# Dividing the first batch's attention output by its sums as it leaves PSUM, with TensorE spreading the reciprocals

## The chip, the core and the metric

The kernel runs on one core of one Trainium2 chip. The metric is the device time of one execution in microseconds (us); lower is better. The core's engines work side by side, each through its own queue in order: PE (TensorE, matrix products), DVE (VectorE), ACT (ScalarE), POOL (GpSimd) and SP (SyncE, which issues the transfers here). SBUF is the on-chip memory, PSUM the small memory that PE writes its results to.

## The reference

Attention with a sliding window and a few sink keys feeds a gated feed-forward network. There are 4 batches, 8 heads, 768 positions and 64 numbers per head.

```python
scores = scale * np.matmul(q, k.transpose(0, 1, 3, 2))
keep = is_sink | in_window                 # 4 sinks, a window of 128
scores = np.where(keep, scores, -1000000000.0)
scores = scores - np.max(scores, axis=-1, keepdims=True)
a = np.exp(scores)
a = a / (np.sum(a, axis=-1, keepdims=True) + 1e-09)
x = np.matmul(a, v)                        # heads side by side: 512 numbers
h = np.maximum(x @ w_in, 0.0)              # 1024 numbers
conv_out = ...                             # 3 taps along the sequence
gate = 1.0 / (1.0 + np.exp(-conv_out))
out = (h * gate) @ w_out
```

The weights w_in, conv_w and w_out come as 64-bit numbers and are narrowed on the chip.

## The kernel before

**Work and its order.** Heads go in pairs; g numbers the 16 pairs of all batches, four to a batch. A sequence has six query tiles of 128, in two halves (hf 0 and 1). The jobs of the first batch are the first halves of its four pairs, then their second halves: 24 steps of one query tile each. Per step the loop in `banded` calls `scores` for this tile, `transp` for the tile before and `pv` for the one two steps back, and between them takes pieces of feed-forward work (`fill`). The feed-forward network of the first 256 positions can start after the 12th step; from then on PE has such pieces between the attention work. One weight block per step, from step 2 to step 18, is narrowed and split (`m.need`). What each engine runs in which order is set in the end by the compiler's own scheduling pass, which reorders instructions within an engine.

**One query tile** (`scores`). PE makes the scores of both heads (tile sc in PSUM, two buffers). DVE puts in the mask and finds the row maximum (L502, L503), ACT takes the exponential into the tile pe and accumulates the row sums in sm (L506), DVE adds the sums up and takes their reciprocal (L508, L509), and POOL multiplies the probabilities by it, one instruction per head (L511). `transp` turns the scaled probabilities over on PE (pts, L526), ACT copies them out (pT, L528), POOL clears what lies outside the window (L530, L532).

**One half of a pair** (`pv`). PE adds the products of pT and the values into px (L567). The sink keys' probabilities of the three tiles, 16 columns for each head and tile (SP), are copied to sk by ACT (L539), turned over (tk, L540), copied to sT (L542) and multiplied with the sinks' values c.vs, into the same px (L570). `xout` writes x to SBUF in two parts whose sum is x: the high part xH by ACT (L345), the rest xL by DVE (L346). The later batches use other sink tiles and keep the scaling on POOL.

**A weight block** (`split`). `narrow` makes 32-bit numbers of the 64-bit ones (ACT L111, DVE L112, L113, L114; tiles stm, three buffers). ACT writes the high part (L121); the low part is a subtraction of two SBUF tiles (L122), for w_in on POOL, for w_out (wo0 to wo7) on DVE.

**Feed-forward.** `first` puts 12 products into ph (L183; the last three need x of the fourth pair), `gate` works on ACT, DVE (L195, L196, L198) and POOL (L200, L201), `second` adds to po (L210). The tag "h" of the PSUM pool has two buffers; ph, tk and the turned q and k tiles share it. In the first batch two SBUF tiles, roomH and roomL, lie where x of the second batch will be; roomH holds zeros and the sinks' values.

## Time and profile before

| | |
|---|---|
| median of 3 runs | 490.8 us (489.17 to 491.21) |
| the profiled execution | 491.53 us; its span is 489.8 us, so 1.73 us lie around the span |
| mean granted PE clock | 0.991 |
| busy over the span | PE 457.6, DVE 343.8, ACT 344.3, POOL 314.0 us |
| PE busy, first 12 us | 2.07 us (loading) |
| PE busy, 12 to 102 us | 76.78 of 90 us (first batch's attention, feed-forward from about 49 us) |
| PE busy, 120 to 360 us | 239.56 of 240 us |
| PE busy, 360 to 490 us | 122.15 of 130 us |

The profile lists every instruction with start and duration. A row "0.5 <-DVE sm L509" gives idle time and what ended it. A view by stages gives busy time of each engine in a stretch, the number of instructions in brackets, and the clock that PE was granted. Ends of matmuls are modelled, so a matmul's own duration is longer than the distance to the next one.

### The profile page before, as it was taken

What the parts mean: (1) busy time and instruction counts of PE and PEld (TensorE: products, weight loads), DVE (VectorE), ACT (ScalarE), POOL (GpSimd) and SP (SyncE); (2) the same over time, 40 slices, a digit from 0 to 9 for tenths busy, and PEclk for the clock granted to TensorE, in tenths of its full rate; (3) what the DMA queues carried; (4) which work ended last, traced back from release to release, by engine and by line L of the source; (5) the groups of instructions that cost most, each with busy time, mean ns of one, the idle gap of its engine ahead of it and who ended that gap; (6) DMA issues with size and microseconds to landing.
All of it is one profiled execution on the core that took longest, in us unless ns stands there. A gap on an engine that the chain in (4) does not pass through costs nothing.

```text
span 489.8 us, 10503 instructions
## 1 busy us (share of the span) xinstructions
PE 457.6 (93%) x3149; PEld 388.8 (79%) x3149; DVE 343.8 (70%) x1211; ACT 344.3 (70%) x1087; POOL 314.0 (64%) x614
## 2 busy tenths in 40 slices
PE   1877698999999999999999999999999999999993
PEld 1644577778888888998888887898888888999982
DVE  4689989857768777776677778686776574655561
ACT  3888877869867978887768877785867664545541
POOL 3396688856876868695657667585765564444341
PEclk9999979999999999999999999999999999999999
DMA  5687744547234141433231421333120100101001
GB/s 145 188 250 205 187 146 84 135 91 184 52 81 115 62 115 33 101 96 83 73 86 35 107 68 34 71 92 85 45 58 8 45 2 1 44 1 43 26 20 51
DMA packets 87307, 41.01 MB, mean 84 GB/s; under 512 B 80161, under 2 KB 80185, under 8 KB 87241
## 3 DMA queue, kind: packets, MB, share of 16 engines
q1 hardware_dynamic: 87240, 40.25, 32.0%
q8 instruction: 27, 0.44, 0.4%
q14 instruction: 40, 0.32, 0.2%
HBM read 27.60 MB, written 6.29 MB: 69 GB/s over the span
## 4 chain that ended last, share of the span: by engine, by line
PE 83%; POOL 4%; DVE 3%; ACT 3%; DMA 3%; issue 2%; SPq 1%; DVEq 0%; ACTq 0%; POOLq 0%
PE ph L183 28%; PE po L210 27%; PE px L567 8%; PE pts L526 4%; PE sc L337 4%; PE sc L338 3%; PE px L570 2%; PE tq L271 2%; POOL pe L511 2%; PE sc L334 2%; PE tk L289 1%; DMA raw<-in_k_dram 1%; POOL wiL L122 1%; DMA sc_i<-in_window_dram 1%; POOL pT L530 1%
## 5 line engine op out<-in xcount | busy, mean ns | idle before, releaser
L210 PE MATMUL po<-woH,g 128*128 128x512 f32 x384 | 142.2, 410 | 1.2 <-POOL g L200 1.2
L183 PE MATMUL ph<-xH,wiH 128*128 128x258 f32 (+1 forms) x384 | 112.7, 293 | 1.2 <-ACT sT L542 1.2
L183 PE MATMUL ph<-xH,wiL 128*128 128x258 f32 (+1 forms) x384 | 110.0, 287 | 0.0
L183 PE MATMUL ph<-xL,wiH 128*128 128x258 f32 (+1 forms) x384 | 109.4, 285 | 0.0
L511 POOL TENSOR_SCALAR pe<-pe,sm 128x132 f32<-128x132 f32 (+1 forms) x192 | 86.0, 459 | 30.4 <-DVE sm L509 19.1
L200 POOL TENSOR_SCALAR g<-t 128x256 fp32r<-128x256 f32 x96 | 41.9, 437 | 79.1 <-DVE t L198 59.0
L506 ACT ACTIVATE pe<-pe,sm 128x132 f32<-128x132 f32 (+1 forms) x192 | 77.5, 407 | 16.6 <-DVE sm L503 15.2
L195 DVE SCALAR_TENSOR_TENSOR t<-hb,cw,t 128x256 f32<-128x256 f32 x96 | 55.5, 579 | 35.5 <-ACT t L194 34.4
L210 PEld LDWEIGHTS po<-woH,g 128*128 128x128 f32 x384 | 69.0, 189 | 12.1 <-POOL g L200 2.6
L183 PEld LDWEIGHTS ph<-xH,wiH 128*128 128x128 f32 x384 | 73.2, 191 | 6.6 <-ACT sT L542 2.0
L201 POOL TENSOR_TENSOR g<-t,g 128x256 fp32r<-128x256 f32 x96 | 74.3, 774 | 5.4
L210 PE MATMUL po<-woL,g 128*128 128x512 f32 x192 | 76.6, 399 | 0.0
L183 PEld LDWEIGHTS ph<-xH,wiL 128*128 128x128 f32 x384 | 73.3, 191 | 2.2
L183 PEld LDWEIGHTS ph<-xL,wiH 128*128 128x128 f32 x384 | 73.3, 191 | 0.9
L197 ACT ACTIVATE t<-t 128x256 f32<-128x256 f32 x96 | 40.3, 420 | 34.7 <-DVE t L196 34.4
L502 DVE COPY_PREDICATED sc<-before,sc 128x128 f32<-128x128 int32 x160 | 44.9, 291 | 25.7 <-PE sc L338 20.5
L198 DVE SCALAR_TENSOR_TENSOR t<-t,hb 128x256 f32<-128x256 f32 x96 | 47.0, 490 | 21.1 <-ACT t L197 20.2
L503 DVE CUSTOM_DVE_ANT_0 pe<-sc,m 128x132 f32<-128x132 f32 (+1 forms) x192 | 52.6, 288 | 10.1 <-PE sc L338 7.8
L196 DVE SCALAR_TENSOR_TENSOR t<-hb,cw,t 128x256 f32<-128x256 f32 x96 | 55.6, 579 | 4.4
L530 POOL TENSOR_SCALAR_AFFINE_SELECT pT<-pT 128x256 f32<-128x256 f32 x80 | 39.2, 490 | 29.5 <-ACT pT L528 25.2
L190 ACT ACTIVATE hb<-ph 128x258 f32<-128x258 f32 (+1 forms) x96 | 37.0, 385 | 29.3 <-PE ph L183 27.8
L194 ACT ACTIVATE t<-hb,cw 128x256 f32<-128x256 f32 x96 | 49.2, 513 | 7.1 <-POOL g L201 3.3
(123 smaller groups left out, 918.4 us busy)
## 6 DMA issues: line engine op xcount, KB each, us to landing
raw<-in_q_dram SPq DMA_DIRECT2D x64, 96.0 KB
raw<-in_k_dram SPq DMA_DIRECT2D x64, 96.0 KB
out_dram<-stm SPq DMA_DIRECT2D x24, 256.0 KB
kk<-kk SPq DMA_DIRECT2D x24, 198.0 KB
vraw<-in_v_dram SPq DMA_DIRECT2D x24, 192.0 KB
wi_0r<-in_moe_w_in_dram SPq DMA_DIRECT2D x2, 512.0 KB
wi_1r<-in_moe_w_in_dram SPq DMA_DIRECT2D x2, 512.0 KB
wi_2r<-in_moe_w_in_dram SPq DMA_DIRECT2D x2, 512.0 KB
```

The costliest lines, as they stand in the source:

```text
L183: nc.tensor.matmul(u.h[:, 0:W], w[:, cc, ff * P:(ff + 1) * P], x[:, cc, t0:t1], start=(i == 0), stop=(i == len(prods) - 1))
L194: nc.scalar.mul(a, prev, cw[:, 0, ff:ff + 1])
L195: nc.vector.scalar_tensor_tensor(out=e, in0=this, scalar=cw[:, 1, ff:ff + 1], in1=a, op0=ALU.mult, op1=ALU.add)
L196: nc.vector.scalar_tensor_tensor(out=a, in0=nxt, scalar=cw[:, 2, ff:ff + 1], in1=e, op0=ALU.mult, op1=ALU.add)
L198: nc.vector.scalar_tensor_tensor(out=a, in0=e, scalar=1.0, in1=this, op0=ALU.add, op1=ALU.mult)
L201: nc.gpsimd.tensor_tensor(out=u.g[:, 1], in0=a, in1=f(u.g[:, 0]), op=ALU.subtract)
L210: nc.tensor.matmul(po[:, 0:c.DM], u.g[:, a, tt * P:(tt + 1) * P], w[:, ff, :], start=(ff == 0 and i == 0), stop=(ff == NFF - 1 and i == 2))
L502: nc.vector.copy_predicated(pc[:, KW:SW], before.bitcast(I32), pc[:, 0:P])
L503: nc.vector.tensor_tensor_reduce(out=pe[:, j, cols], in0=pc[:, P:SW][:, cols], in1=mk, op0=ALU.add, op1=ALU.min, scale=1.0, scalar=3.0e38, ...
L506: nc.scalar.activation(pe[:, j, cols], pe[:, j, cols], AF.Exp, bias=sm[:, j:j + 1], scale=-1.0, accum_out=sm[:, 2 + 2 * j:3 + 2 * j])
L511: nc.gpsimd.tensor_scalar(pe[:, j, cols], pe[:, j, cols], sm[:, 8 + j:9 + j], 1.0, ALU.mult, ALU.mult)
L530: nc.gpsimd.affine_select(out=keytile(g, t - 1, hf)[:, :, 1], in_=own, pattern=[[0, 2], [-1, P]], compare_op=ALU.is_gt, fill=c.zero, base= ...
```

## The change

For the first batch (g below 4) only:

- `scores` no longer multiplies the probabilities on POOL (L511, 48 instructions). The reciprocals are written as a fifth column beside the four sink columns of sk (SP is 5 instead of 16), one column for each head and tile, so sk has 30 columns instead of 96.
- sk is turned over as before; sT then holds, besides the sinks' unscaled probabilities, the reciprocals of the three tiles along the free axis. A constant c.sel (made once by ACT in roomL) has ones in those rows that belong to the reciprocals of one tile. Three further products of c.sel and sT per half put into rb, a PSUM tile of tag "h", the reciprocal for each of the 128 rows of px and each position: 24 matmuls.
- `xout` copies rb to a part of roomL by ACT, DVE multiplies px by it into the same place, and xH and xL are made from there instead of from px: per half one ACT and one DVE instruction more.
- The rows of c.vs that are not sinks are zero, so the reciprocal columns add nothing to px.

For all weights: the low parts of wo0 to wo7 are subtracted on POOL instead of DVE.

```diff
-SP = 16
+SP = NS + 1
...
-                out.append((f"wo{ff}", ..., lambda raw, ff=ff: self.split(..., self.c.nc.vector)))
+                out.append((f"wo{ff}", ..., lambda raw, ff=ff: self.split(..., self.c.nc.gpsimd)))
...
-    def xout(self, g, half, px):
+    def xout(self, g, half, px, rb=None):
...
+        if rb is not None:
+            n = 384 * (1 + g % 2)
+            r = c.room[:, n:n + 384]
+            nc.scalar.copy(r, rb)
+            nc.vector.tensor_tensor(out=r, in0=px, in1=r, op=ALU.mult)
+            px = r
         nc.scalar.copy(xH[:, hp, s], px)
         nc.vector.tensor_tensor(out=xL[:, hp, s], in0=px, in1=f(xH[:, hp, s]), op=ALU.subtract)
...
+    c.room = m.room[1]
+    c.sel = m.room[1][0:6 * SP, 0:3 * P].rearrange("r (w p) -> r w p", w=3)
+    nc.scalar.copy(c.sel.rearrange("r w (j d) -> r (w j) d", j=2),
+                   c.ident[0:6 * SP, NS:6 * SP:SP].rearrange("r (n o) -> r n o", o=1).to_broadcast([6 * SP, 6, D]))
...
         nc.vector.tensor_reduce(out=sm[:, 6:8], ...)
+        if g < NPAIR:
+            if u == 0:
+                s.sk[hf] = ap.tile([P, 6, SP], F32, tag="sk", name=f"sk{g}_{hf}")
+            nc.vector.reciprocal(s.sk[hf][:, 2 * u:2 * u + 2, NS], sm[:, 6:8])
+            return
         nc.vector.reciprocal(sm[:, 8:10], sm[:, 6:8])
...
-                sk = ap.tile([P, 6, SP], F32, tag="sk", name=f"sk{g}_{hf}")
-                nc.scalar.copy(sk, sinks[:, :, 0:SP])
+                sk = s.sk[hf]
+                nc.scalar.copy(sk[:, :, 0:NS], sinks[:, :, 0:NS])
...
-        A.xout(g, hf, px)
+        rb = None
+        if g < NPAIR:
+            rb = m.ps.tile([P, 3 * P], F32, tag="h", name=f"rb{g}_{hf}", bufs=2)
+            for w in range(3):
+                nc.tensor.matmul(rb[:, P * w:P * w + P], c.sel[:, w], s.sT, start=True, stop=True, skip_group_check=True)
+        A.xout(g, hf, px, rb)
```

The change shifts line numbers by 6 to 20; L511 of before is L526 after, L530 and L532 are L545 and L547, L502 and L503 are L512 and L513, L346 is L352.

The order of the instructions moves with it. In the rows below the last number of a name is a buffer's number, and "0" or "1" ahead of it the half. First, POOL's queue while the first halves of the first batch run, before; pe are probabilities, wiL and woL low parts of weights, pT the turned probabilities:

```order
L122 TENSOR_TENSOR wiL<-stm_329,wiH 128x512
L511 TENSOR_SCALAR pe_0_421<-pe_0_421,sm_160 128x128 x2
L511 TENSOR_SCALAR pe_0_421<-pe_0_421,sm_161 128x132 x2
L122 TENSOR_TENSOR wiL<-stm_380,wiH 128x512
L530 AFFINE_SELECT pT_0_0_355<-pT_1_0_406 128x2x128
L493 MEMSET pe_0_545 128x2x4
L530 AFFINE_SELECT pT_1_0_406<-pT_2_0_437 128x2x128
L511 TENSOR_SCALAR pe_0_421<-pe_0_421,sm_162 128x132 x2
L532 AFFINE_SELECT pT_1_0_406<-pT_1_0_406 128x2x128
L532 AFFINE_SELECT pT_2_0_437<-pT_2_0_437 128x2x128
```

The same stretch of POOL's queue after:

```order
L122 TENSOR_TENSOR wiL<-stm_323,wiH 128x512
L122 TENSOR_TENSOR wiL<-stm_378,wiH 128x512
L545 AFFINE_SELECT pT_0_0_347<-pT_1_0_402 128x2x128
L503 MEMSET pe_0_541 128x2x4
L547 AFFINE_SELECT pT_1_0_402<-pT_1_0_402 128x2x128
L545 AFFINE_SELECT pT_1_0_402<-pT_2_0_432 128x2x128
L547 AFFINE_SELECT pT_2_0_432<-pT_2_0_432 128x2x128
L122 TENSOR_TENSOR woL<-stm_448,woH 128x512
L545 AFFINE_SELECT pT_0_0_472<-pT_1_0_527 128x2x128
L547 AFFINE_SELECT pT_1_0_527<-pT_1_0_527 128x2x128
L122 TENSOR_TENSOR woL<-stm_503,woH 128x512
```

The scalings are gone, and subtractions of w_out stand between the window clearings.

Second, DVE's queue where the first pair's second half ends and the second pair's begins, before; sc are scores, t the gate's tiles, sm the sums:

```order
L195 SCALAR_TENSOR_TENSOR t_802<-hb_114,cw,t_801 128x256
L112 TENSOR_SCALAR stm_704<-stm_705 128x512
L502 COPY_PREDICATED sc_3_0_827<-before,sc_3_0_827 128x128
L508 TENSOR_REDUCE sm_163<-sm_163 128x2
L196 SCALAR_TENSOR_TENSOR t_801<-hb_114,cw,t_802 128x256
L113 SCALAR_TENSOR_TENSOR stm_704<-wi_2r,stm_704 128x512
L502 COPY_PREDICATED sc_3_1_828<-before,sc_3_1_828 128x128
L503 ISA pe_1_826,sm_159<-sc_3_0_827,m_135 128x132
```

The same place of DVE's queue after (roomL takes the product of px and the reciprocals):

```order
L113 SCALAR_TENSOR_TENSOR stm_760<-wi_3r,stm_760 128x512
L349 TENSOR_TENSOR roomL<-px_0_727,roomL 128x384
L518 TENSOR_REDUCE sm_164<-sm_164 128x2
L114 SCALAR_TENSOR_TENSOR stm_760<-stm_761,stm_760 128x512
L522 RECIPROCAL sk_1_678<-sm_164 128x2
L512 COPY_PREDICATED sc_3_0_823<-before,sc_3_0_823 128x128
L352 TENSOR_TENSOR xL_117<-roomL,xH_116 128x384
L512 COPY_PREDICATED sc_3_1_824<-before,sc_3_1_824 128x128
L513 ISA pe_1_822,sm_160<-sc_3_0_823,m_135 128x132
```

The gate's first instruction is the 196th of DVE's queue instead of the 175th and has left this place; x of the fourth pair (from px_0_727) is finished here, as the 183rd, where before it was the 166th, ahead of the rows shown.

Third, PE's queue at the end of the first feed-forward unit (ph_746), before; X and kk are turned q and k:

```order
L570 MATMUL px_0_735<-sT_0_695,roomH 128x128 x2
L334 MATMUL sc_5_0_772<-kk_174,X_575 128x260
L313 MATMUL trk_751<-ident,raw_70 128x128 x3
L334 MATMUL sc_5_1_773<-kk_174,X_575 128x260
L526 MATMUL pts<-ident,pe_1_670 128x128 x2
L183 MATMUL ph_746<-xH_116,wiH 128x258
L183 MATMUL ph_746<-xH_116,wiL 128x258
L183 MATMUL ph_746<-xL_117,wiH 128x258
```

PE's queue after, where that unit (ph_744) and the second one (ph_807) end:

```order
L334 MATMUL sc_3_0_823<-kk_175,X_695 128x260
L183 MATMUL ph_807<-xL_117,wiH 128x258
L541 MATMUL pts<-ident,pe_1_666 128x128
L334 MATMUL sc_3_1_824<-kk_175,X_695 128x260
L541 MATMUL pts<-ident,pe_1_666 128x128
L183 MATMUL ph_744<-xH_116,wiH 128x258
L183 MATMUL ph_744<-xH_116,wiL 128x258
L183 MATMUL ph_807<-xH_116,wiH 128x258
L183 MATMUL ph_807<-xH_116,wiL 128x258
L183 MATMUL ph_744<-xL_117,wiH 128x258
L183 MATMUL ph_807<-xL_117,wiH 128x258
```

The products with the fourth pair's x, which close a unit, stand behind the scores of the next pair's fourth tile (sc_3) now; before they stood ahead of them.

More of the change, by code (lines that the diff above doesn't have):

```diff
@@ L143, in weights @@
             for ff in range(HF * half, HF * half + HF):
-                out.append((f"wo{ff}", vo[:, ff, :], lambda raw, ff=ff: self.split(raw, self.wo, (slice(None), ff), self.c.nc.vector)))
+                out.append((f"wo{ff}", vo[:, ff, :], lambda raw, ff=ff: self.split(raw, self.wo, (slice(None), ff), self.c.nc.gpsimd)))
         self.place = {x[0]: i for i, x in enumerate(out)}
@@ L454, in banded @@
     for s in st:
-        s.pe, s.pT, s.raw, s.X = {}, {}, {}, [None, None]
+        s.pe, s.pT, s.sk, s.raw, s.X = {}, {}, {}, {}, [None, None]
     st[0].v = c.v_raw[0]
```

## The prediction

> **What bounds the kernel now.** I read the stages first, to see where PE, the busiest engine, is not full; then what the engines wait for there, then the durations of what is removed and added. In the view by stages (start and end, length, busy time and count of each engine, granted clock) the reader sees three parts:
>
> ```profile
> core 0: us, PE busy (x) PEld busy (x) DVE busy (x) ACT busy (x) POOL busy (x), PEclk, DMA share, GB/s
> 24.00:96.00 72.00, 60.00 (x358) 43.67 (x358) 65.68 (x216) 58.55 (x183) 57.60 (x93) 0.95 0.64 170
> 12.00:102.00 90.00, 76.78 (x448) 56.46 (x447) 77.02 (x266) 72.34 (x225) 66.60 (x110) 0.96 0.62 164
> 96.00:120.00 24.00, 23.02 (x176) 19.96 (x175) 14.95 (x70) 18.42 (x64) 14.18 (x31) 1.00 0.60 145
> 120.00:360.00 240.00, 239.56 (x1762) 207.60 (x1761) 177.04 (x675) 186.43 (x620) 173.31 (x348) 1.00 0.31 76
> 360.00:490.00 130.00, 122.15 (x809) 107.93 (x807) 72.54 (x193) 67.46 (x186) 60.47 (x113) 0.99 0.08 25
> ```
>
> From 96 to 360 us PE is full, and the change touches nothing there. So the end moves as the moment moves at which the first batch's attention is over (102 us) and PE has all its feed-forward work ahead of it. In the 90 us before, PE idles 90 - 76.78 = 13.2 us. From 24 to 96 us DVE is the fullest engine, 65.68 of 72 (91%), ahead of PE with 60.00, ACT with 58.55 and POOL with 57.60. DVE paces this stage, and the others hold it up where they make it wait. The waits of 12 to 102 us (who, for whom, us in total, times, longest):
>
> ```profile
> PEld pts L526 <- POOL pe L511: 6.0, 9, 1.2
> ACT sk L539 <- POOL pe L511: 4.1, 4, 1.9
> DVE sc L502 <- PE sc L334: 3.5, 6, 1.2
> PE sc L334 <- DVE sm L509: 3.5, 1, 3.5
> ```
>
> PE and ACT wait 10.1 us for the scaling on POOL, and DVE's largest wait, 3.5 us for scores, is behind PE. One stop of PE stands out; the timeline around it:
>
> ```profile
> 57.23 1.26 POOL L122 TENSOR_TENSOR wiL<-stm,wiH 128x512 fp32r<-128x512 f32 x1 [0.52 <-ACT wiH L121]
> 57.51 1.27 DVE L196 SCALAR_TENSOR_TENSOR t<-hb,cw,t 128x256 f32<-128x256 f32 x1
> 58.70 0.89 DVE L113 SCALAR_TENSOR_TENSOR stm<-wi_2r,stm 128x512 int32<-128x512 int32 x1
> 60.15 0.68 PE L334 MATMUL sc<-kk,X 128*128 128x260 f32 x2 [3.47 <-DVE sm L509]
> 61.63 0.47 DVE L196 SCALAR_TENSOR_TENSOR t<-hb,cw,t 128x256 f32<-128x256 f32 x1
> ```
>
> PE needs a score tile that DVE frees only after L196 and L113, and idles 3.47 us. The clock then falls, in the stages behind it:
>
> ```profile
> 62.00:64.00 2.00, 2.00 (x6) 1.25 (x6) 1.69 (x8) 1.50 (x7) 2.00 (x3) 0.50 0.25 100
> 64.00:66.00 2.00, 2.00 (x9) 1.68 (x8) 2.00 (x6) 1.14 (x3) 2.00 (x4) 0.50 0.06 25
> 66.00:68.00 2.00, 2.00 (x12) 1.97 (x11) 1.02 (x4) 0.53 (x3) 2.00 (x5) 0.62 0.63 238
> ```
>
> At half clock PE is full and DVE idles 0.31 + 0.98 = 1.3 us: for these microseconds PE is the bound. The Trainium skill, "TensorE: Matmul & The Clock Gate", section "What's actually happening", has the clock halved after an idle window of about 3.4 us; the trace agrees with 3.47 us here. By that page a gap somewhat shorter would cost no clock at all.
>
> **The change, part by part.** Durations, from the groups of the first 110 us (busy, mean ns, idle before):
>
> ```profile
> L511 POOL TENSOR_SCALAR pe<-pe,sm 128x132 f32<-128x132 f32 x40 | 22.3, 569 | 11.9 <-DVE sm L509 7.4 <-ACT X L250 2.4 <-ACT xH L345 2.1
> L122 POOL TENSOR_TENSOR wiL<-stm,wiH 128x512 fp32r<-128x512 f32 x8 | 10.4, 1304 | 5.7 <-ACT wiH L121 5.7
> L122 DVE TENSOR_TENSOR woL<-stm,woH 128x512 fp32r<-128x512 f32 x8 | 5.9, 733 | 0.4 <-ACT woH L121 0.4
> L346 DVE TENSOR_TENSOR xL<-px,xH 128x384 fp32r<-128x384 f32 x7 | 3.8, 545 | 1.3 <-ACT xH L345 1.3
> L250 ACT ACTIVATE kk<-trk 128x384 f32<-128x384 f32 x8 | 3.9, 489 | 2.8 <-PE trk L313 2.8
> L539 ACT COPY sk<-pe 128x96 f32<-128x96 f32 x8 | 2.2, 273 | 4.1 <-POOL pe L511 4.1
> L322 ACT COPY kk<-kk 128x24 f32<-128x24 f32 x4 | 0.8, 210 | 0.0
> L511 POOL TENSOR_SCALAR pe<-pe,sm 128x128 f32<-128x128 f32 x9 | 3.9, 440 | 1.1 <-DVE sm L509 1.1
> ```
>
> 1. DVE's own work. It loses eight subtractions of w_out, 8 x 733 ns = 5.9 us, and gains eight multiplications of px, with the shape of L346: 8 x 545 ns = 4.4 us. The reciprocals stay, and xL keeps its size. Net -1.5 us on the engine that paces the stage.
>
> 2. POOL. It loses 40 x 569 + 8 x 440 ns = 26.3 us and gains 8 x 1304 ns = 10.4 us: 15.9 us less, of 66.60. This is no time by itself, but POOL and DVE slow each other: L196 took 1.27 us beside the subtraction L122 on POOL and 0.47 us without. For the six L196 between 24 and 96 us, and two neighbours:
>
> ```profile
> L196 DVE SCALAR_TENSOR_TENSOR t<-hb,cw,t 128x256 f32<-128x256 f32 x6 | 5.5, 921 | 0.0
> L195 DVE SCALAR_TENSOR_TENSOR t<-hb,cw,t 128x256 f32<-128x256 f32 x6 | 3.6, 604 | 1.4 <-ACT t L194 1.4
> L198 DVE SCALAR_TENSOR_TENSOR t<-t,hb 128x256 f32<-128x256 f32 x6 | 3.3, 552 | 0.0
> ```
>
> Against 470 ns these lost (451 + 134 + 82) x 6 = 4.0 us. With POOL's work down by a quarter I take a quarter back, -1.0 us. The ends: all of it back, -4.0; or each new subtraction on POOL holds one instruction of DVE as L196 was held, 8 x 0.80 = +6.4.
>
> 3. The waits for POOL. Transposes and the sink copy now follow the exponential directly. Of the 13.2 us of PE's idle time and the 24 to 96 us idle time of DVE, 72 - 65.68 = 6.3 us, the second counts, since DVE paces. 1.3 us of it belong to the slow clock (below); of the other 5.0 I take two fifths, -2.0, since of DVE's waits only the 3.5 us for PE lie behind POOL, and ACT stands in that chain too. Ends 0 and -5.0. What is late next: ACT, with 8 x 489 ns = 3.9 us for the copies of rb, less 8 x 63 ns for the narrower sk, so +3.4 us. Its 58.55 of 72 leaves room for that, and the making of c.sel (at most another 489 ns) falls into the loading. If that cover is gone, the whole 3.4 us come on top. Queued behind the rb copy on ACT are exponentials that DVE's sums wait for; the copy's own input needs sT, which is ready before px is.
>
> 4. The stop of PE and the clock. In the order after, the gate's L196 no longer stands between the scores and L503 there: instead of 1.27 + 0.89 us DVE has one xL of 0.55 and a multiplication of 0.55. I take the clock to stay up: -1.3 us, DVE's idle time at half clock. Ends 0 (the gap returns elsewhere) and PE's side of it, 2 x (0.50 + 0.50 + 0.38) = 2.8 us of lost clock in the three rows, -2.8.
>
> 5. PE. 24 more products of the kind of L570. In the chain of waits four of them take 0.64 us:
>
> ```profile
> 51.71 0.64 PE px L570 x4
> ```
>
> so 0.16 us each, 3.8 us in all. 18 of them lie inside the stage, hidden by PE's idle time (13.2 us; without it they would cost 2.9 us). The six of the last two halves come after 96 us, where PE is full: +1.0 us. One PSUM tile of tag "h" more per half can hold up a q or k transpose for an ACT copy, 0.5 us; hidden by the same idle time.
>
> Sum: -1.5 - 1.0 - 2.0 - 1.3 + 1.0 = -4.8 us. The profiled execution took 491.53 us (span 489.8), 0.7 above the median of 490.8; taken from the median the sum gives 486.0 us.
>
> **The rivals.** A measurement of this kernel tells about 0.5%, 2.45 us, from no change.
>
> No change: POOL's subtractions hold DVE. Term 2 at its upper end, the rest as above: -1.5 + 6.4 - 2.0 - 1.3 + 1.0 = +2.6; with two of eight missing a victim, +1.0, 491.8 us. For it speaks the L196 row, against it that most of DVE's instructions in a step work on scores in PSUM, and that 48 instructions which also read SBUF leave POOL. The Trainium skill, "SBUF — State Buffer", section "SBUF: two separate sides", speaks against the change: an instruction of DVE with two SBUF inputs and one of POOL that reads SBUF share an exclusive lock, and the loser waits for the whole of the other. By that rule a new subtraction could hold DVE for 1.30 us, eight of them 10.4 us, and the sum would be +6.6; the row (0.80 us lost) shows a good part of that wait. The same rule credits the 48 scalings that go.
>
> Slower: x is late, and PE has nothing to do. Each half now needs a multiplication (545 ns) between px and the high part, and the order after finishes the fourth pair's x 17 rows later in DVE's queue and the first gate 21 rows later. PE's queue holds the last products of both first units behind that x, and everything behind them. If what POOL gave back is lost so, PE's idle time stays at 13.2 us and all 24 products come on top: +3.8 us, 494.6. It decides from the point where PE's idle time in the stage falls by less than 3.8 us, to more than 9.4. Against it: the 10.1 us of waiting for POOL are gone for certain.
>
> Much faster: PE, not DVE, turns out to pace the stage. Then half of PE's idle time goes, 6.6, and the clock's 2.8, less 1.0: -8.4, 482.4 us. For it speak the many waits of PE in the list; against it DVE's 91%.
>
> **How the numbers follow.** Forecast, 483 to 488.3 us: 0.50. Much faster, below 483: 0.10. No change, within 2.45 us: 0.25, since term 2 can turn over the sum. Slower: 0.15. Faster is then 0.60, same 0.25, slower 0.15. The predicted time is the forecast's 486.0. The range from 480.5 (just past the much faster case) to 493.0 (the end of no change) leaves out the slower case and a little of the first.
>
> **What would show it.** Term 1: DVE's L122 rows gone, eight multiplications near 545 ns. Term 2: L195, L196 and L198 in the stage nearer 470 ns; POOL's w_out subtractions near 1.3 us. Term 3: pts and sk wait for ACT, not POOL, and DVE's share in the stage stays at 90% or more while the stage is shorter. Term 4: no PE gap of 3.4 us and no stretch at clock 0.50. Term 5: 24 more matmuls, PE's idle time between 12 us and the last px of the first batch near 7 us (97.2 - 12 us less 76.8 + 3.8 - 2.5 us of work). The prediction is wrong if that last px (now at 102 us) does not come near 97, if DVE's busy time there rises, or if PE gaps appear at ph with ACT's xH or DVE's xL as releaser.

## The result, and the profile after

The changed kernel took 497.3 us (median of 4 runs, 496.4 to 499.0) against 490.8 before: 1.0139 times as long, 95% interval 1.0117 to 1.0161. It is slower by some 6.5 us, where 4.8 us less were forecast; the time lies above the range. The profiled execution took 497.6 us, its span is 495.8 us (before 491.5 and 489.8), and its mean granted clock is 0.982 (before 0.991).

The stages, and from the page the busy time of the engines and the chain that ended last:

```profile
24.00:96.00 72.00, 64.57 (x375) 48.98 (x375) 63.66 (x195) 55.80 (x173) 48.13 (x58) 0.91 0.60 163
12.00:102.00 90.00, 80.80 (x462) 60.94 (x462) 77.11 (x264) 71.41 (x228) 53.60 (x68) 0.92 0.60 164
120.00:360.00 240.00, 237.17 (x1739) 205.28 (x1738) 178.15 (x666) 182.79 (x616) 170.01 (x343) 1.00 0.30 75
```

```profile
PE 466.9 (94%) x3197; PEld 396.9 (80%) x3197; DVE 350.6 (71%) x1211; ACT 344.1 (69%) x1096; POOL 301.8 (61%) x574
PE 79%; DVE 7%; DMA 5%; ACT 3%; issue 2%; SPq 1%; POOL 1%; DVEq 0%; ACTq 0%; POOLq 0%
```

POOL's share of the chain fell from 4% to 1%, DVE's rose from 3% to 7%. The books of PE: the span is 6.0 us longer. Its idle time (span less busy) fell from 32.2 to 28.9, -3.3 us. The time lost to the clock, (1 - clock) x span, rose from 4.4 to 8.9, +4.5 us. The rest of the added busy time, 9.3 - 4.5 = +4.8 us, goes with the 48 records more (x3149 before).

What the engines ran up to 110 us, after:

```profile
L114 DVE SCALAR_TENSOR_TENSOR stm<-stm,stm 128x512 int32<-128x512 int32 x16 | 14.4, 901 | 0.1
L122 POOL TENSOR_TENSOR woL<-stm,woH 128x512 fp32r<-128x512 f32 x8 | 11.6, 1452 | 7.3 <-ACT woH L121 7.3
L112 DVE TENSOR_SCALAR stm<-stm 128x512 int32<-128x512 int32 x16 | 10.6, 661 | 2.3 <-ACT stm L111 2.0 <-ACT pe L516 0.4
L591 PE MATMUL rb<-sT,roomL 30*128 30x128 f32 x42 | 6.8, 300 | 0.0
L349 DVE TENSOR_TENSOR roomL<-px,roomL 128x384 f32<-128x384 f32 x7 | 3.8, 547 | 0.0
L348 ACT COPY roomL<-rb 128x384 f32<-128x384 f32 x7 | 3.3, 469 | 1.5 <-PE rb L591 1.5
```

and two of these groups before, which the prediction did not show:

```profile
L114 DVE SCALAR_TENSOR_TENSOR stm<-stm,stm 128x512 int32<-128x512 int32 x16 | 11.2, 698 | 0.0
L112 DVE TENSOR_SCALAR stm<-stm 128x512 int32<-128x512 int32 x16 | 7.6, 477 | 1.8 <-ACT stm L111 1.6
```

These two lines of the narrowing of the weights on DVE take 16 x (203 + 184) ns = 6.2 us longer; the third, L113, is 0.8 us shorter in all (758 instead of 809 ns in the mean of 16 blocks). The timeline shows where, and what follows on PE (four engines, put in order of time):

```profile
37.52 1.74 POOL L122 TENSOR_TENSOR woL<-stm,woH 128x512 fp32r<-128x512 f32 x1 [3.36 <-ACT woH L121]
38.16 1.65 DVE L114 SCALAR_TENSOR_TENSOR stm<-stm,stm 128x512 int32<-128x512 int32 x1
39.29 0.69 ACT L111 ACTIVATE stm<-wo2r 128x512 f32<-128x512 f32 x1 [0.67 <-POOL woL L122]
40.39 1.03 ACT L250 ACTIVATE X<-trq,headscale 128x384 f32<-128x384 f32 x2
40.57 1.26 POOL L122 TENSOR_TENSOR woL<-stm,woH 128x512 fp32r<-128x512 f32 x1
40.66 1.46 DVE L112 TENSOR_SCALAR stm<-stm 128x512 int32<-128x512 int32 x1
41.48 0.55 PE L313 MATMUL trk<-ident,raw 128*128 128x128 f32 x3 [1.05 <-ACT X L250]
41.73 0.47 ACT L348 COPY roomL<-rb 128x384 f32<-128x384 f32 x1
42.10 0.38 ACT L543 COPY pT<-pts 128x256 f32<-128x256 f32 x1
42.53 0.44 PE L541 MATMUL pts<-ident,pe 128*128 128x128 f32 x2 [0.51 <-DMA raw<-in_q_dram]
42.55 0.86 POOL L545 TENSOR_SCALAR_AFFINE_SELECT pT<-pT 128x256 f32<-128x256 f32 x1 [0.72 <-ACT pT L543]
44.27 1.99 PE L582 MATMUL px<-pT,vraw 128*64 128x128 f32 x12 [1.30 <-POOL pT L547]
```

The two narrowings shown end 0.55 and 0.29 us after the subtraction on POOL beside them (39.81 behind 39.26, 42.12 behind 41.83), as if DVE had waited for POOL's whole instruction. Not every one is held: an L112 of 0.41 us began at 44.81 us, 0.03 us after a subtraction of 1.56 us. PE stops three times in four microseconds, and as the rows show it the way to these stops goes by ACT's queue. ACT's L111 waits 0.67 us until POOL's subtraction is over; L250, which the first stop waits for, runs behind it; the copy of rb (L348) and L543 run behind that. The second stop ends with L543 (its own row names a DMA, but PE's weight load ahead of it waited 0.74 us for L543), and the third with the selections on POOL, which begin when L543 is done. The chain that ended last, however, runs by DVE's narrowings from 34.5 to 47.6 us, so the profile does not settle which of the two ways counts. The clock then falls (in the stages, the number ahead of the last two is the clock):

```profile
42.00:44.00 2.00, 0.46 (x3) 0.20 (x2) 1.97 (x8) 2.00 (x8) 1.38 (x2) 1.00 0.29 72
44.00:46.00 2.00, 1.73 (x12) 0.90 (x12) 1.93 (x5) 1.09 (x4) 1.44 (x2) 0.69 0.81 241
50.00:52.00 2.00, 1.19 (x5) 0.82 (x4) 2.00 (x7) 1.32 (x6) 1.27 (x2) 0.50 0.16 29
58.00:60.00 2.00, 2.00 (x15) 1.59 (x15) 1.13 (x6) 1.17 (x3) 1.19 (x2) 0.90 0.04 8
```

From about 45 to 58 us PE runs at half speed; before it did so from about 61 to 67.5. What the feed-forward work waits for is x. The high parts of the fourth pair's two halves, before and after:

```profile
52.39 0.48 ACT L345 CAST xH<-px 128x384 fp32r<-128x384 f32 x1 [0.38 <-PE px L570]
111.99 0.48 ACT L345 CAST xH<-px 128x384 fp32r<-128x384 f32 x1 [0.34 <-PE px L570]
```

```profile
62.76 0.51 ACT L351 CAST xH<-roomL 128x384 fp32r<-128x384 f32 x1 [0.62 <-DVE roomL L349]
118.56 0.51 ACT L351 CAST xH<-roomL 128x384 fp32r<-128x384 f32 x1 [1.50 <-DVE roomL L349]
```

The first is 10.4 us late, the last 6.6, about the loss of the whole span (6.0). Most of the 10.4 us lies ahead of this half's own copy and multiplication. The last products into its px, before and after, and after the copy of its rb:

```profile
51.64 0.71 PE L570 MATMUL px<-sT,roomH 96*128 96x128 f32 x4
```

```profile
54.78 0.48 ACT L348 COPY roomL<-rb 128x384 f32<-128x384 f32 x1 [0.76 <-PE rb L591]
60.98 0.71 PE L585 MATMUL px<-sT,roomH 30*128 30x128 f32 x4
```

px is done at 52.35 us before and at 61.69 after, 9.3 us late, while its rb had been copied at 55.26. At the second pair the changed kernel was still ahead (36.89 us instead of 39.54). So it loses its time in the first batch, between the second pair and the fourth, as the prediction's "Slower" rival has it, and the question is which part of the change makes x late.

### The profile page after: what moved, and what is told of

It is laid out like the page before. It is cut to its first block, busy times and chain, and to the rows that moved or that the text cites. A ratio compares the mean times of both kernels' runs of the same rounds, so it can differ in the third digit from the quotient of the medians.

```text
span 495.8 us, 10535 instructions
## 1 busy us (share of the span) xinstructions
PE 466.9 (94%) x3197; PEld 396.9 (80%) x3197; DVE 350.6 (71%) x1211; ACT 344.1 (69%) x1096; POOL 301.8 (61%) x574
## 4 chain that ended last, share of the span: by engine, by line
PE 79%; DVE 7%; DMA 5%; ACT 3%; issue 2%; SPq 1%; POOL 1%; DVEq 0%; ACTq 0%; POOLq 0%
PE ph L183 26%; PE po L210 26%; PE px L582 7%; PE pts L541 4%; PE sc L337 3%; PE sc L338 3%; PE sc L334 3%; PE px L585 2%; PE tq L271 2%; PE tk L289 2%; DVE stm L113 1%; DVE stm L114 1%; DMA wi_2r<-in_moe_w_in_dram 1%; DMA wo0r<-in_moe_w_out_dram 1%; DMA raw<-in_k_dram 1%
## 5 line engine op out<-in xcount | busy, mean ns | idle before, releaser
L210 PE MATMUL po<-woH,g 128*128 128x512 f32 x384 | 140.6, 405 | 2.6 <-POOL g L200 2.6
L195 DVE SCALAR_TENSOR_TENSOR t<-hb,cw,t 128x256 f32<-128x256 f32 x96 | 57.2, 595 | 36.9 <-ACT t L194 35.9
L210 PEld LDWEIGHTS po<-woH,g 128*128 128x128 f32 x384 | 68.7, 188 | 12.9 <-POOL g L200 3.7
L526 POOL TENSOR_SCALAR pe<-pe,sm 128x132 f32<-128x132 f32 (+1 forms) x144 | 60.6, 431 | 29.4 <-DVE sm L524 22.9
L513 DVE CUSTOM_DVE_ANT_0 pe<-sc,m 128x132 f32<-128x132 f32 (+1 forms) x192 | 52.7, 287 | 15.4 <-PE sc L338 11.4
L198 DVE SCALAR_TENSOR_TENSOR t<-t,hb 128x256 f32<-128x256 f32 x96 | 49.9, 520 | 17.5 <-ACT t L197 16.8
L512 DVE COPY_PREDICATED sc<-before,sc 128x128 f32<-128x128 int32 x160 | 44.7, 290 | 22.8 <-PE sc L338 16.1
L545 POOL TENSOR_SCALAR_AFFINE_SELECT pT<-pT 128x256 f32<-128x256 f32 x80 | 38.6, 483 | 32.9 <-ACT pT L543 31.6
L196 DVE SCALAR_TENSOR_TENSOR t<-hb,cw,t 128x256 f32<-128x256 f32 x96 | 54.1, 563 | 4.5
```

The costliest lines, as they stand in the source:

```text
L195: nc.vector.scalar_tensor_tensor(out=e, in0=this, scalar=cw[:, 1, ff:ff + 1], in1=a, op0=ALU.mult, op1=ALU.add)
L196: nc.vector.scalar_tensor_tensor(out=a, in0=nxt, scalar=cw[:, 2, ff:ff + 1], in1=e, op0=ALU.mult, op1=ALU.add)
L198: nc.vector.scalar_tensor_tensor(out=a, in0=e, scalar=1.0, in1=this, op0=ALU.add, op1=ALU.mult)
L210: nc.tensor.matmul(po[:, 0:c.DM], u.g[:, a, tt * P:(tt + 1) * P], w[:, ff, :], start=(ff == 0 and i == 0), stop=(ff == NFF - 1 and i == 2))
L512: nc.vector.copy_predicated(pc[:, KW:SW], before.bitcast(I32), pc[:, 0:P])
L513: nc.vector.tensor_tensor_reduce(out=pe[:, j, cols], in0=pc[:, P:SW][:, cols], in1=mk, op0=ALU.add, op1=ALU.min, scale=1.0, scalar=3.0e38, ...
```

## The experiments

Ratios are to the kernel before, run beside each kernel on the same chip; its median there was 490.4 to 491.2 us. All diffs are against the changed kernel unless said otherwise.

### One part alone

**division_only.** The low parts of wo back on DVE:

```diff
-... self.split(raw, self.wo, (slice(None), ff), self.c.nc.gpsimd)
+... self.split(raw, self.wo, (slice(None), ff), self.c.nc.vector)
```

> The division by products of TensorE as in the changed kernel; w_out's low parts stay on DVE. Theory A (the 24 products of the spreading are 48 passes of PE, about 0.14 us each, 6.8 us, and PE has no room for them): the time stays at 496 to 498 us, since PE's work is the same. Rival B (the subtractions on POOL hold DVE's narrowing, L112 and L114, which grew from 477 and 698 to 661 and 901 ns): these two fall back below 520 and 730 ns and the time falls to 492 to 494 us. Rival C (the clock: a stop of PE near 42 us and 14 us at half clock behind it): the stop goes with the order, PE's mean clock rises from 0.982 to 0.99 and the time falls by 2 to 3 us.

Measured: 493.2 us, 1.0055 (1.0036 to 1.0075). The ten runs lie in two groups: 490.5 and 490.8 us with a granted clock of 0.997, eight from 493.0 to 495.1 with 0.982 to 0.991. L112 and L114 fell back to 520 and 740 ns, near the bounds that rival B gave (520 and 730). The profiled run is of the first group; the three stops at 41 to 44 us are one:

```profile
41.04 0.44 PE L541 MATMUL pts<-ident,pe 128*128 128x128 f32 x2 [1.02 <-ACT pT L543]
```

The division alone costs some 2.7 us. The two runs at 0.997 take the time of the kernel before, whose own runs show a clock of 0.984 to 0.996, so rival C has a part in it too.

**wo_low_on_pool_only.** The kernel before, with the low parts of wo on POOL:

> The kernel before with w_out's low parts on POOL and nothing else. Theory A: within 1.5 us of 490.8, since PE's work is unchanged. Rival B: L112 and L114 on DVE slow down as in the changed kernel and the time rises by 2 to 4 us, to 493 to 495.

Measured: 493.0 us, 1.0045 (1.0030 to 1.0060): 2.2 us lost, though DVE has 5.9 us less to do. Rival B, then. Narrowing slowed too (L112 596 ns, L114 770 ns). The stage (24 to 96 us) had DVE less busy than before, 59.67 instead of 65.68 us:

```profile
24.00:96.00 72.00, 59.73 (x340) 44.06 (x339) 59.67 (x191) 53.46 (x170) 61.75 (x90) 0.88 0.59 160
```

**no_spreading.** No products, no copy, no multiplication:

```diff
-        if g < NPAIR:
+        if False:
             rb = m.ps.tile([P, 3 * P], F32, tag="h", ...)
```

> The changed kernel without the 24 products, without the copy of rb on ACT and without the multiplication on DVE; the first batch's x is not divided. It shows what taking the scaling off POOL is worth by itself, with w_out's low parts on POOL. Theory A: the 6.8 us of PE are gone and POOL's relief remains: 487 to 490.5 us, faster than the kernel before. Rival B: the subtractions on POOL still cost their 2 to 4 us, so 493 to 495 us. Rival D (x comes late by the multiplication and the copy): x is early again, the first ph product near 49 us instead of 55 us, and the time falls to 488 to 491 us too; it differs from A in the run with the products doubled.

Measured: 488.6 us, 0.9967 (0.9951 to 0.9984). The spreading as a whole is worth 497.3 - 488.6 = 8.7 us. Narrowing is slower here than in the changed kernel (672 and 937 ns against 661 and 901), and the time is shorter than before:

```profile
L114 DVE SCALAR_TENSOR_TENSOR stm<-stm,stm 128x512 int32<-128x512 int32 x16 | 15.0, 937 | 0.1
L112 DVE TENSOR_SCALAR stm<-stm 128x512 int32<-128x512 int32 x16 | 10.7, 672 | 0.5 <-ACT stm L111 0.4
```

So long narrowings alone do not make the loss.

**spreading_twice.** Each of the 24 products issued twice:

```diff
-            for w in range(3):
+            for w in (0, 1, 2, 0, 1, 2):
```

> The changed kernel with each of the 24 products made twice into the same tile; the values are the same. Theory A: PE is full, so another 48 passes cost their whole 6.8 us: 502 to 505 us. Rival D (x is late, PE's room is there): PE's idle time takes most of it and the time rises by less than 2.5 us, to 497 to 500 us.

Measured: 496.2 us, 1.0116 (1.0094 to 1.0139), not slower than with 24:

```profile
L591 PE MATMUL rb<-sT,roomL 30*128 30x128 f32 x96 | 12.5, 275 | 0.0
```

PE has 48 records more than the changed kernel, but in all four runs the clock shows 0.994 to 0.997, and the profile has no half clock between 36 and 72 us. By the books of PE the added work (8.7 us more than in the changed kernel's profile, with the clock's part taken out) is offset by 7.4 us less lost to the clock and 2.4 us less idle time. Theory A falls; rival D's 497 to 500 was missed by less than 1 us.

**products_alone.** The kernel before, with c.sel and the 24 products added, rb read by nobody:

```diff
+        if g < NPAIR:
+            rb = m.ps.tile([P, 3 * P], F32, tag="h", name=f"rb{g}_{hf}", bufs=2)
+            for w in range(3):
+                nc.tensor.matmul(rb[:, P * w:P * w + P], c.sel[:, w], s.sT, ...)
```

> The kernel before, and the 24 spreading products added with nothing else: their result is read by nobody, so that no instruction of another engine is added but the one that makes the matrix of ones. 48 passes, 6.6 to 6.8 us on PE. Theory A (PE has too little idle time that others don't need: its 13.2 us of idle time up to 102 us are waits inside a chain, which the products lengthen): 493 to 497. Rival (the products fill idle time as the prediction had it, with 6 of 24 of them outside): 490.7 to 492. If the added work keeps PE busy where it stopped before (60 us), the clock shows 0.995 or more and the time can come out under 490.7.

Measured: 491.6 us, 1.0027 (1.0010 to 1.0044), +1.3 us. Theory A falls: PE's idle time does hide the products.

### The clock and the buffer

**kept_warm.** Products of the first halves of pairs 2 and 3 (counted from 0) issued twice:

```diff
-            for w in range(3):
+            for w in ((0, 1, 2, 0, 1, 2) if hf == 0 and g > 1 else (0, 1, 2)):
```

> The changed kernel, with the spreading products of the first halves of pairs 2 and 3 issued twice: 6 products more, 12 passes of 0.14 us, so 1.7 us more work on PE, all of it ahead of the stops at 41 to 45 us. Theory C (the stops at 41 to 45 us put PE at half clock for some 14 us, and that is most of what the change loses): the added work fills the stops, the clock stays near 1.00 (0.99 or more over the run) and the time falls to 492 to 495 although PE has more to do. Rival A (PE's own work is the loss, the clock costs next to nothing because PE waits for others there): the time rises by 0 to 1.7 to 497 to 499, whatever the clock does.

Measured: 500.5 us, 1.0209 (1.0162 to 1.0257), by both theories' numbers a miss. The added work did not fill the stops; the profile still shows two of 1.15 and 1.26 us at 42 and 44 us and half clock from 42 to 56. So it does not test theory C. Its four runs do show that time and clock go together: 496.3 us at 0.985, 499.1 at 0.981, 501.8 and 502.1 at 0.970 and 0.969. Two numbers speak against the clock as the main loss: the changed kernel's run of 496.4 us had a clock of 0.988, with which runs of the kernel before took 490.3 to 492.7 us, and spreading_twice took 496.2 us at 0.997.

**rb_beside_h.** rb of the first halves in another PSUM buffer:

```diff
-            rb = m.ps.tile([P, 3 * P], F32, tag="h", ...)
+            rb = m.ps.tile([P, 3 * P], F32, tag="h" if hf else "po", ...)
```

> The changed kernel, with the spread reciprocals of the first halves in the other double buffer of PSUM (that of the FFN's second products, idle early) instead of the one that the transposes of q and k take. Theory D (the stop of 1.05 us at 41.5 us, where q's transposes wait for a buffer that the spread reciprocals hold, starts the half clock): the stop is gone, the clock is 0.99 or more, 492 to 495. Rival (the stops come from VectorE and GpSimd being late with the weights, and the buffer only shows it): stops of the same length with another releaser, 496 to 498.

Measured: 501.4 us, 1.0195 (1.0129 to 1.0261). The stop at 41 us is gone, others of 0.8 and 1.2 us come at 44 and 46 us, and half clock lasts from 48 to 65 us. Theory D falls: the half clock comes without that wait. The rival's time (496 to 498) was missed too; why this kernel is slower still is open.

**one_pass_products.** The low parts of wo on DVE, reciprocals split in a high and a low column, a second, rounded copy of the turned block (sR):

```diff
-SP = NS + 1
+SP = NS + 2
...
-                nc.tensor.matmul(rb[:, P * w:P * w + P], c.sel[:, w], s.sT, ...)
+                nc.tensor.matmul(rb[:, P * w:P * w + P], c.sel[:, w], s.sR, ...)
```

> The changed kernel with the low parts of wo back on VectorE, and each spreading product in one pass: the reciprocals are split in a high and a low column (two small VectorE instructions for each half), and ScalarE makes a second copy of the transposed block, rounded for the one-pass type. PE does 24 passes for the spreading instead of 48, some 3.4 us less. Theory A (PE's passes are the loss of the division): 488.5 to 490.8, under the 493.2 of the division with two passes. Rival C (the division's loss is the clock after a stop, which does not depend on the passes): 490.5 to 493.5, in the two groups of before, by whether the clock shows 0.997 or 0.988. Rival E (the small instructions added, 16 on VectorE of some 0.15 us and 8 on ScalarE of some 0.3 us, eat the gain): 492 to 494 at any clock.

Measured: 492.4 us, 1.0046 (1.0024 to 1.0067), as division_only within the error. PE ran half the records:

```profile
L600 PE MATMUL rb<-sR,sel 36*128 36x128 f32 x24 | 4.3, 286 | 0.3 <-ACT sR L566 0.3
```

Half the passes on PE brought less than 1 us, so theory A falls; that the small instructions added ate a gain (rival E) is not excluded. All ten runs show a clock of 0.984 to 0.992.

### What of the low parts on POOL costs

Four kernels change what POOL does in the eight instructions for w_out (w is the narrowed block, H its high part, L the low part):

```diff
-        engine.tensor_tensor(out=L, in0=w, in1=f(H), op=ALU.subtract)
+            engine.tensor_tensor(out=L, in0=w, in1=w, op=ALU.subtract)             # two_inputs_no_wait
+            engine.tensor_scalar(L, w, 2.0 ** -12, 1.0, ALU.mult, ALU.mult)        # one_input_no_wait
+            engine.tensor_scalar(L, f(H), 2.0 ** -12, 1.0, ALU.mult, ALU.mult)     # one_input_wait
+            engine.memset(f(L), 0.0)                                               # no_input
```

> The changed kernel, in which GpSimd makes the low parts of wo from the narrowed weights alone (w minus w, so that the low parts are zero and the output differs): two inputs as before, but no wait for ScalarE's high parts. Theory B1 (GpSimd's two-input instruction slows VectorE's narrowing beside it: the two lines of narrowing at 661 and 901 ns instead of 520 and 740, and that makes the stops at 41 to 45 us): as the changed kernel, 496 to 499, the two lines above 620 and 860 ns. Theory B2 (GpSimd takes its queue in order, and the 7.3 us that it waits for ScalarE's high parts hold the selections that PE needs): 493 to 495.5, the stop that waits for GpSimd's selection at 44 us is gone.

> The changed kernel, in which GpSimd makes the low parts of wo as the narrowed weights times a constant (the output differs): one input, no wait for ScalarE's high parts. Theory B1: the two lines of narrowing come down to 480 to 560 and 690 to 780 ns, 493 to 495.5. Theory B2: the same time, by the wait that is gone, with the two lines where they are in the changed kernel. Rival (neither matters, the loss is PE's products alone): 496 to 499.

> The changed kernel, in which GpSimd makes the low parts of wo as the high parts times a constant (the output differs): one input, and the wait for ScalarE's high parts as it is. Theory B1: the two lines of narrowing at 480 to 560 and 690 to 780 ns, 493 to 495.5. Theory B2: 496 to 499, GpSimd waits some 7 us for the high parts, and the stop for the selection at 44 us stays.

> The changed kernel, in which GpSimd writes zeros as the low parts of wo (the output differs): no input, no wait. It bounds what these eight instructions can cost. Theory B1: the two lines of narrowing at 420 to 520 and 680 to 740 ns, 492 to 494.5, since only the division's products are left of the loss (493.2 with the low parts on VectorE). Theory A (the products alone make the loss): 496 to 499.

Measured, in this order: 498.9 us (1.0158 to 1.0204), 492.6 (1.0028 to 1.0060), 496.6 (1.0075 to 1.0132; single runs from 493.9 to 502.6), 502.7 (1.0214 to 1.0287). The instructions, one row from each kernel's groups in the same order:

```profile
L123 POOL TENSOR_TENSOR woL<-stm 128x512 fp32r<-128x512 f32 x8 | 9.2, 1153 | 6.6 <-DVE stm L114 3.4 <-DVE sk L525 3.3
```

```profile
L123 POOL TENSOR_SCALAR woL<-stm 128x512 fp32r<-128x512 f32 x8 | 5.5, 683 | 10.1 <-DVE stm L114 5.6 <-DVE sk L525 4.3
```

```profile
L123 POOL TENSOR_SCALAR woL<-woH 128x512 fp32r<-128x512 f32 x8 | 7.5, 939 | 6.3 <-ACT woH L121 6.0
```

```profile
L123 POOL MEMSET woL<- 128x512 f32 x8 | 3.7, 514 | 0.0
```

The wait for ACT alone is not it: without it and with two inputs the time is no better (498.9). One input alone is not it either: with the wait it takes 496.6, where theory B2 put it. The short instruction without the wait brings the time to that of division_only (492.6 and 493.2), so these eight instructions, as they stand in the change, make a loss of 4 to 5 us. Which way it goes is only half shown: L112 and L114 came down to 581 and 761 ns in one_input_no_wait, near theory B1's 560 and within its 780, but L114 is at 734 ns in two_inputs_no_wait too, against B1's number, and no_spreading was fast with longer ones. B1 and B2 each fail in some of the four, and how these instructions cost their time stays open. no_input does not bound the cost as meant: a memset has nothing to wait for, so the eight of them ran together in the loading, and there they held DVE. The first row is POOL's, the other DVE's:

```profile
9.77 3.74 POOL L123 MEMSET woL<- 128x512 f32 x8
...
9.70 3.84 DVE L431 COPY m<-stm 128x4 f32<-128x4 f32 x1
```

In one_input_no_wait the same copy takes

```profile
9.70 0.16 DVE L431 COPY m<-stm 128x4 f32<-128x4 f32 x1
```

PE's first scores then came 5.7 us later (17.6 instead of 11.9 us).

### What of the spreading costs

products_alone had left a question: why does the spreading cost 8.7 us, when its products cost 1.3? Three kernels take it apart (multiply_only multiplies by zeros, which lie in SBUF from the start; no run shows whether an x of zeros changes the time of what follows):

```diff
-            rb = m.ps.tile(...)                                    # copy_multiply_only: no products
+            rb = px
...
-            rb = m.ps.tile(...)                                    # products_unread: xout gets no rb
+            rq = m.ps.tile(...)
...
-            nc.scalar.copy(r, rb)                                  # multiply_only: no products, no copy
-            nc.vector.tensor_tensor(out=r, in0=px, in1=r, op=ALU.mult)
+            nc.vector.tensor_tensor(out=r, in0=px, in1=self.zeros[:, 0:384], op=ALU.mult)
```

**scaling_gone_only** is division_only without all three. **turned_over_swapped** turns over the two heads of a pair in the other order, `for j in (1, 0)`, and changes nothing else but what the scheduling pass makes of it.

> The changed kernel without the 24 spreading products and their PSUM tile: ScalarE copies px itself, and VectorE multiplies px by that copy, so the two instructions per half stay, with the same shapes, and x is wrong. Theory F (the copy and the multiplication, a longer chain from px to x on the two engines that pace the stage, make the loss): 494.5 to 498. Theory A (the products on PE make it): 488 to 490.5. Both in part: 491 to 494.

> The changed kernel with the 24 spreading products, but their result read by nobody: no copy on ScalarE, no multiplication on VectorE, x undivided. Theory A (the products): 494.5 to 498. Theory F (copy and multiplication): 489 to 491, that is 488.6 without any spreading and about the 1.2 us that the products cost in the kernel before. Both in part: 491 to 494.

> The kernel before with GpSimd's scaling left out and nothing in its place: low parts of wo on VectorE, no spreading, x undivided. It gives the gain that the division can pay for. If the parts add up (low parts of wo on GpSimd cost 2.2, no spreading with them gave 488.6): 486 to 487. If the gain is small because VectorE paces the stage and has 5.9 us more to do here than with the low parts on GpSimd: 488 to 490.

> The changed kernel, in which the two heads of a pair are turned over in the other order in the first batch: the same instructions, the same work, but the scheduling pass puts some hundred instructions in another order. Theory G (a good part of the differences of 2 to 4 us between these kernels is the order alone): off 497.3 by more than 1.5 us, most likely below, with another stop and another length at half clock. Rival (the order moves little; the parts make the times): 496 to 498.5.

> The changed kernel without the spreading products and without ScalarE's copy: VectorE multiplies px by a block of zeros in SBUF, with the same shapes, so x is wrong. Theory F1 (VectorE's multiplication, on the engine that paces the stage, and what stands behind it make the 7.0 us): 493 to 496. Theory F2 (ScalarE's copy, which stands in its queue between exponentials, makes most of it): 489 to 491.5.

| kernel | us | ratio, 95% interval |
|---|---|---|
| scaling_gone_only | 486.2 | 0.9897 (0.9880 to 0.9915) |
| no_spreading (the same, low parts of wo on POOL) | 488.6 | 0.9967 (0.9951 to 0.9984) |
| multiply_only (and the multiplication) | 488.7 | 0.9978 (0.9961 to 0.9995) |
| copy_multiply_only (and the copy) | 495.6 | 1.0096 (1.0074 to 1.0119) |
| the changed kernel (and the products) | 497.3 | 1.0139 (1.0117 to 1.0161) |
| products_unread (no_spreading and the products) | 490.4 | 0.9984 (0.9971 to 0.9998) |
| turned_over_swapped | 496.8 | 1.0109 (1.0085 to 1.0132) |

Down the first five rows each step adds one part. In us of 490.8, each known to about 1.2: the scaling gone -5.1, the low parts of wo on POOL +3.4, the multiplication +0.5, the copy +5.8, the products +2.1. Together +6.7. The error is that of the runs alone. Kernels that differ little from the changed one lie between 1.5 us below it (turned_over_swapped) and 3.4 above (kept_warm, with 6 products more), so a step of 2 us may be order or clock. The large steps come out alike in other pairs: the low parts on POOL +2.2 (wo_low_on_pool_only), +3.4 and +4.1 (the changed kernel against division_only), and the copy with the multiplication +6.3 here and +7.6 from products_unread to the changed kernel. The products alone come out at +0.8 (products_unread against no_spreading), +1.3 and +2.1.

Theory F is right in its size (495.6 us) and theory A wrong in both kernels; F1 is wrong, F2 right: with ACT's copy comes the cost, with DVE's multiplication alone it does not. The copy step has two things in it, ACT's instruction and the multiplication's wait for it, and no run parts them; in copy_multiply_only the copy reads px and so always runs behind it, in the changed kernel it reads rb. In the stage DVE is fuller with the multiplication alone than in any other kernel, and only 0.5 us is lost; multiply_only first, then copy_multiply_only:

```profile
24.00:96.00 72.00, 59.22 (x363) 43.98 (x364) 70.42 (x216) 56.81 (x183) 50.78 (x63) 0.98 0.62 169
```

```profile
24.00:96.00 72.00, 60.46 (x352) 45.15 (x352) 69.54 (x206) 57.16 (x181) 48.56 (x60) 0.93 0.63 167
```

The copies take 3.7 us of ACT, and with them the time grows by 5.8. In the profile the loss stands as stops of PE again, two of them before the fourth pair's x, each for a score buffer that DVE frees behind a long narrowing; one of them, where the narrowing ends 0.55 us after POOL's subtraction:

```profile
57.29 1.26 POOL L122 TENSOR_TENSOR wiL<-stm,wiH 128x512 fp32r<-128x512 f32 x1 [0.47 <-ACT wiH L121]
57.48 1.62 DVE L113 SCALAR_TENSOR_TENSOR stm<-wi_2r,stm 128x512 int32<-128x512 int32 x1
59.46 1.20 PE L334 MATMUL sc<-kk,X 128*128 128x260 f32 x2 [1.87 <-DVE sm L513]
```

multiply_only has narrowings as long as that (1.75 and 1.74 us, at 45.9 and 53.8 us), but PE had feed-forward products to run there, since x came earlier. That this is how the copy's time grows is read from two profiles, not shown by an experiment, and the two kernels differ in the pass's order as well. The one change of order without a change of work, turned_over_swapped, moved the changed kernel by 0.5 us by the medians and 1.5 by the ratios; theory G, that the order makes these differences, asked for more than 1.5 and is neither borne out nor excluded.

**low_part_on_gpsimd.** division_only, with xL of the first batch made by POOL:

```diff
-        nc.vector.tensor_tensor(out=xL[:, hp, s], in0=px, in1=f(xH[:, hp, s]), op=ALU.subtract)
+        (nc.vector if rb is None else nc.gpsimd).tensor_tensor(out=xL[:, hp, s], in0=px, in1=f(xH[:, hp, s]), op=ALU.subtract)
```

> The division with the low parts of wo on VectorE (493.2 before), and GpSimd instead of VectorE makes the low part of x in the first batch: 8 instructions of 0.59 to 0.76 us off VectorE, 8 of about 1.04 us (GpSimd's subtraction of the same width, for q) on GpSimd, which has 43 of 90 us idle. Theory F1 (VectorE's time is what the stage pays): 488.5 to 491. Rival (GpSimd's two-input subtractions slow VectorE by as much as they relieve it, as the low parts of wo did): 493 to 495.

Measured: 495.3 us, 1.0096 (1.0067 to 1.0125), some 2 us slower than division_only: the rival. Even in the profiled run, the fastest (491.5 us), PE waits for POOL's part itself:

```profile
60.99 0.51 PE L183 MATMUL ph<-xL,wiH 128*128 128x258 f32 x2 [1.37 <-POOL xL L352]
```

No kernel that computes the whole output beats the one before.

## Why the prediction was wrong, point by point

The sum by parts, in us (measured by the steps above):

| part | forecast | measured |
|---|---|---|
| the scaling gone (terms 2 to 4) | -4.3 | -5.1 |
| the subtractions of w_out to POOL (in term 1) | -5.9 | +3.4 |
| the multiplication on DVE (in term 1) | +4.4 | +0.5 |
| the copy on ACT (in term 3) | 0 | +5.8 |
| the products (term 5) | +1.0 | +2.1 |

Two steps turned the sum: the credit for the subtractions, and the copy that was put at nothing.

**That DVE paces the stage**, so that work taken off it or put on it counts at its full length, is the step that failed first; the other terms were built on it. It was read from DVE's busy share (91%), and a busy row can hold time in which DVE waits for POOL. In the kernel before, the chain that ended last, read for 24 to 96 us alone, has POOL's scaling as its largest line (L511, 12.9%) and no line of DVE above 3.5%; in no_spreading and multiply_only, where the scaling is gone and POOL subtracts for w_out, DVE's narrowings have the largest shares of any line (L114 11.1 and 13.6%, L113 10.9 and 14.4%), and both are faster than before. 4.4 us more on DVE (multiply_only) cost 0.5 us; 5.9 us less (wo_low_on_pool_only) gained none and lost 2.2. The moment of the fourth pair's x sorts the kernels better (profiled executions):

| kernel | xH of its first half, us | time, us |
|---|---|---|
| scaling_gone_only | 50.2 | 486.6 |
| multiply_only | 50.3 | 488.4 |
| no_spreading | 51.8 | 488.2 |
| before | 52.4 | 491.5 |
| division_only | 53.8 | 490.8 |
| one_input_no_wait | 59.4 | 492.4 |
| copy_multiply_only | 60.3 | 494.9 |
| changed | 62.8 | 497.6 |
| rb_beside_h | 63.6 | 503.2 |

It is no law (one_pass_products has 50.0 and 492.2, spreading_twice 55.5 and 496.4, kept_warm 63.7 and 496.3), and it does not say what makes x late, but it is what the feed-forward work starts on.

**Term 1** (-1.5) had the multiplication's length right, 545 ns forecast and 547 measured, and its cost wrong, +0.5 instead of +4.4. The 5.9 us of subtractions that DVE lost brought nothing: moving them cost 2.2 us alone and 3.4 with the scaling gone.

**Term 2** (-1.0, ends -4.0 and +6.4) was mis-sized and looked at the wrong victims. L195, L196 and L198 in the stage:

```profile
L195 DVE SCALAR_TENSOR_TENSOR t<-hb,cw,t 128x256 f32<-128x256 f32 x5 | 3.8, 750 | 0.0
L198 DVE SCALAR_TENSOR_TENSOR t<-t,hb 128x256 f32<-128x256 f32 x5 | 2.9, 579 | 0.0
L196 DVE SCALAR_TENSOR_TENSOR t<-hb,cw,t 128x256 f32<-128x256 f32 x5 | 2.7, 541 | 0.0
```

L196 fell from 921 to 541 ns, L195 rose from 604 to 750, L198 from 552 to 579: together 0.2 us less for each round of the gate. But subtractions of w_out on POOL fall beside narrowings on DVE, and L112 and L114 lost 6.2 us, nearly the upper end. The Trainium skill's lock ("SBUF — State Buffer", section "SBUF: two separate sides"), by which DVE waits for the whole of POOL's instruction, agrees with the two narrowings shown (0.55 and 0.29 us behind POOL's end); the 0.80 us that the prediction put against it was one collision, in which L196 had begun 0.28 us behind POOL. That these 6.2 us are what the time lost does not follow, as no_spreading shows.

**Term 3** (-2.0). The waits for the scaling went, and that was worth more than forecast: the scaling alone gone gave -5.1 us, against -4.3 for terms 2 to 4. (Of the 10.1 us of waiting that it read, 6.0 are those of PE's weight loads, which overlap the products; the products' own wait was 2.1 us.) ACT's cover did not hold, though: the prediction priced that at "the whole 3.4 us", and the time grew by 5.8 with the copy. An engine at 58.55 of 72 us was taken to have room. It has, on average; the copy still stands in its queue ahead of other work, as at 41.73 us, where L543 and two of PE's stops come behind it. That this makes the 5.8 us is read from the profile; the runs show the size, not the way.

**Term 4** (-1.3). The 3.47-us stop at 60 us went, as forecast, and three shorter ones came at 41 to 44 us, with twice the time at half clock: 4.5 us more lost to the clock in the profile, where the term's ends were 0 and -2.8.

**Term 5** (+1.0) came out at +0.8 (products_unread), +1.3 (products_alone) or +2.1, about its size by luck, since two of its steps were wrong. A product of this type is two records, so the row x4 was two products, and 24 of them fill 7.6 us, not 3.8 (x48 at 296 ns each, overlapping). And the stage ends with the last half's px at 112 us, not at 102, which is the half before. The idle time hid most of the products all the same. The hold-up of a transpose, priced at 0.5 us and hidden, is a stop of 1.05 us in the profile; without it (rb_beside_h) the time was no better.

**The rivals.** "Slower: x is late" is what happened; by its own test, PE's idle time from 12 to 102 us fell by 4.0 us (13.2 to 9.2), a hair past its 3.8, but part of the busy time that took its place was half clock. Its price, 3.8 us for the products, was the wrong item, so that its 494.6 us came nearest to 497.3 partly by luck; what the runs show to cost the time are the copy and the low parts. "No change" had DVE's lost time right (+6.4 forecast, 6.2 in L112 and L114), but not that the copy would cost.

## What to carry to other kernels

A busy share does not say what an engine would do with less work: before pricing work moved off an engine, see whether the chain of that stage runs by it, whether its long rows stand beside another engine's, and whether the result that others wait for (here x of the fourth pair) comes earlier. Here a subtraction on GpSimd also lengthened VectorE's instructions beside it, so that VectorE did not gain what was taken off it. An engine that has room on average can still be late where an instruction is added: the eight copies were 3.7 us of ScalarE's time, and 5.8 us were lost with them.

## What the runs showed of the hardware

- **A run of POOL's instructions held DVE to its end.** In no_input eight memsets of POOL in a row took 3.74 us, and a copy of 128 x 4 numbers on DVE took 3.84 instead of 0.16 us, to 0.03 us behind them. The memsets have no input.
- **GpSimd's length by inputs**, 128 x 512 numbers: 514 ns with none, 683 and 939 with one, 1153 with the same block twice, 1452 with two blocks. These are means of eight and may hold waiting.
- **Half clock without a long stop.** The prediction tied it to one gap of 3.47 us. After, stops of 1.05, 0.51 and 1.30 us between 40.4 and 44.3 us were enough; one stop of 1.41 us (spreading_twice) or 1.02 us (division_only) was not. Half clock then lasted some 14 us, past a further stop of 0.81 us at 51.5 us. The Trainium skill, "TensorE: Matmul & The Clock Gate", section "What's actually happening", has the clock halved after an idle window of about 3.4 us; the trace agrees only in part, since between 42 and 44 us PE was busy for 0.46 us and the clock fell all the same.
- **Runs of one kernel differ with it.** division_only took 490.5 and 490.8 us at a clock of 0.997 and 493 us or more at 0.991 and below.
